# The first chunks of a gated linear attention: order of loads, decays, multiplies and small loads

## The chip, the cores and the metric

The kernel runs on one core of a Trainium2 chip. The metric is the device time of one execution in microseconds; before the change it is 438.04 (median of three runs, 437.43 to 438.84). The engines of the core work in parallel, each in its own program order, and wait for one another through semaphores: TensorE (PE in the profile, with PEld for its weight loads), VectorE (DVE), ScalarE (ACT), GpSimd (POOL), and SyncE (SP), which here only issues DMAs. ScalarE issues some DMAs too; issue work shows as ACTq and SPq.

## The reference

Two blocks follow each other. The first is a gated recurrence over 768 steps for 4 batches and 8 heads of width 48; the second sends every row to the best of 8 experts.

```python
# attention: q, k, v, alpha are (4, 8, 768, 48) float32
for t in range(S):
    state = alpha[:, :, t, :, None] * state + np.einsum('bhd,bhe->bhde', k[:, :, t], v[:, :, t])
    y[:, :, t] = np.einsum('bhd,bhde->bhe', q[:, :, t], state)
x = y.transpose(0, 2, 1, 3).reshape(3072, 384)

# experts: the best of 8 by x @ w_gate, then a two-layer network of that expert
h = np.maximum(x_sorted[lo:hi] @ w1[e], 0.0)      # w1[e]: 384 x 1024
y_sorted[lo:hi] = h @ w2[e]                       # w2[e]: 1024 x 384
out = gate_w[:, None] * y_sorted[inv_perm]
```

## The kernel before

The 3072 rows are cut into 24 chunks of 128. Within a chunk the product of the alphas up to a step is the exponential of a running sum of logarithms. So a chunk goes through these steps:

- `logs`: ScalarE takes the logarithm of alpha.
- `cums`: TensorE sums it along the steps with a triangular matrix ([...]two records each); ScalarE takes exponentials with both signs.
- `operands`: k and q are multiplied by these.
- `transposes`: TensorE transposes both products, ScalarE and VectorE copy them out of PSUM.
- `scores`: TensorE multiplies them, VectorE and ScalarE with GpSimd mask the results.
- `attend`: TensorE adds the earlier state's part, the chunk's own part, and forms the next state.
- `rows`: TensorE turns the result into rows and gate logits.

The last row of the positive exponential, the decay over the whole chunk, is stored to DRAM and loaded back with its elements on other partitions (`Eb`): `decay_out` and `decay_in`, both issued by ScalarE.

```python
def load(n, s):
    ...
    if n == "v":
        st[s][n] = vb[s % len(vb)]
        nc.sync.dma_start(st[s][n][:, :, :D], src)
    else:
        st[s][n] = ld.tile([C, H, D], F32, name=n + "_sb", bufs=5)
        nc.sync.dma_start(st[s][n][:], src)

def loads(s):
    load("k", s + 1)
    load("q", s + 1)
    load("a", s + 2)
    load("v", s)

def logs(s):
    st[s]["ln"] = work.tile([C, H, D], F32, name="ln")
    nc.scalar.activation(st[s]["ln"][:], st[s]["a"][:], AF.Ln)

def cums(s):
    d = st[s]
    cum = rps.tile([C, Dm], F32, name="cum")          # one buffer (rps has bufs=1)
    nc.tensor.matmul(cum[:], lhsT=cmask[:], rhs=d["ln"][:], start=True, stop=True)
    ...
    nc.scalar.activation(d["icp"][:], cum[:], AF.Exp, scale=-1.0)
    nc.scalar.activation(d["cp"][:], cum[:], AF.Exp)

def decay_out(s):
    if s % NB + 1 < NB:
        nc.scalar.dma_start(e_d[s : s + 1, :], st[s]["cp"][C - 1 : C, :])

def decay_in(s):
    ...
        for a in range(2):
            nc.scalar.dma_start(
                d["E"][a * DP : a * DP + D, :], e_d[s].rearrange("(p a d) -> a d p", a=2, d=D)[a],
            )

def operands(s):
    ...
    nc.gpsimd.tensor_tensor(kq[:, 0, :, :D], d["k"][:], heads(d["icp"]), op=ALU.mult)
    nc.gpsimd.tensor_tensor(kq[:, 1, :, :D], d["q"][:], heads(d["cp"]), op=ALU.mult)

def scores(s):
    ...                                               # matmuls into sA and sB
    nc.vector.tensor_tensor(d["dA"][:], sA[:], cmask[:, None, :].to_broadcast([C, NP, C]), op=ALU.mult)
    nc.scalar.copy(d["dB"][:], sB[:])
    nc.gpsimd.affine_select(d["dB"][:], d["dB"][:], ...)

def keep_busy(n):                                     # n matmuls on zeros, to fill idle time
    ...

# the start
for a in range(2):
    for ps_ in (slice(0, NP // 2), slice(NP // 2, NP)):
        ...
        nc.scalar.dma_start(gate[r0 : r0 + D, ps_], ...)      # four small loads
nc.scalar.preload_act_table_set("natural_log_exp_and_others")
for n in "akq":
    load(n, 0)
load("a", 1)
loads(0)
first_consts()
keep_busy(4)
parts = fetch_parts(0)
hots = []
for s in range(-4, NT - 1):
    if s + 5 < NT:
        loads(s + 5)
    do(attend, s)
    do(scores, s + 1)
    ...
    do(cums, s + 3)
    keep_busy({-3: 3}.get(s, 0))
    do(operands, s + 3)
    ...
    do(transposes, s + 2)
    keep_busy({-2: 2}.get(s, 0))
    if s == -1:
        back_consts()
    do(rows, s)
    do(keep_rows, s)
    do(decay_out, s + 3)
    do(decay_in, s + 2)
    do(logs, s + 4)
    ...
```

`do(f, i)` calls `f(i)` where chunk i exists, so the loop's first four turns fill a pipeline.

Of the kernel before, what the change touches and what calls it, by code (L numbers as in the profile page):

```python
# [13 lines left out]
ALU = mybir.AluOpType  # L14
# [4 lines left out]
def kernel(  # L19
# [28 lines left out]
    nc = tc.nc  # L48
    B, H, S, D = q.shape
# [3 lines left out]
    NT = N // C  # L53
# [42 lines left out]
    def at(p, a):  # L96
        return DP * (a ^ (p >= NP // 2))
# [14 lines left out]
    def first_consts():  # L112
        nc.vector.memset(still[:], 0.0)
        make_upper_triangular(nc, cmask[:], 1.0, diag=True)
        make_identity(nc, ident[:])
        nc.gpsimd.memset(back[:], 0.0)
        for t in kqb:
            nc.vector.memset(t[:, :, :, D:], 0.0)
        for t in vb:
            nc.vector.memset(t[:, :, D:], 0.0)  # L120
        for t in Ub + Eb:
            nc.vector.memset(t[:], 0.0)

    def back_consts():

        for ps_ in (slice(0, NP // 2), slice(NP // 2, NP)):
            for a in range(2):
                r0 = at(ps_.start, a)
                r = slice(r0, r0 + D)
                nc.vector.tensor_copy(  # L130
                    back[r, ps_, a * D : (a + 1) * D], ident[r, None, r0 : r0 + D].to_broadcast([D, NP // 2, D]),
                )
                nc.vector.tensor_scalar_mul(back[r, ps_, D2:], gate[r, ps_, :], -1.0)
# [100 lines left out]
    def fetch_parts(ex):  # L234

        w1 = wpools[0].tile([C, DB, F], F32, name="w1")
        w2 = wpools[0].tile([C, FB, Dm], F32, name="w2")
        w_t[ex] = w1, w2
        for a in range(DB):
            for c in range(0, F, 2 * C):  # L240
                nc.sync.dma_start(w1[:, a, c : c + 2 * C], moe_w1[ex, a * C : (a + 1) * C, c : c + 2 * C])
                yield
        for f in range(FB):
            nc.sync.dma_start(w2[:, f, :], moe_w2[ex, f * C : (f + 1) * C, :])
            yield
# [30 lines left out]
    with tc.tile_pool(name="ld", bufs=6) as ld, \  # L276
# [5 lines left out]
        def rows_of(t, s):  # L282
            b, c = s // NB, s % NB
            return t[b, :, c * C : (c + 1) * C, :].rearrange("h p d -> p h d")

        def load(n, s):
            if s >= NT:
                return
            src = rows_of({"a": alpha, "k": k, "q": q, "v": v}[n], s)
# [17 lines that stand above are left out]
        def pair(t, p):  # L307
            return t[:, 2 * p : 2 * p + 2, :].rearrange("s h d -> s (h d)")

        def heads(t):  # L310
            return t[:].rearrange("s (h d) -> s h d", h=H)

        def cums(s):
            d = st[s]
            cum = rps.tile([C, Dm], F32, name="cum")
            nc.tensor.matmul(cum[:], lhsT=cmask[:], rhs=d["ln"][:], start=True, stop=True)  # L316
            d["icp"] = work.tile([C, Dm], F32, name="icp")
            d["cp"] = work.tile([C, Dm], F32, name="cp", bufs=3)
# [11 lines that stand above are left out]
                d["E"] = Eb[s % len(Eb)]  # L330
                for a in range(2):
                    nc.scalar.dma_start(
                        d["E"][a * DP : a * DP + D, :], e_d[s].rearrange("(p a d) -> a d p", a=2, d=D)[a],
                    )

        def operands(s):
            d = st[s]
            kq = kqb[s % 4]
            nc.gpsimd.tensor_tensor(kq[:, 0, :, :D], d["k"][:], heads(d["icp"]), op=ALU.mult)  # L339
            nc.gpsimd.tensor_tensor(kq[:, 1, :, :D], d["q"][:], heads(d["cp"]), op=ALU.mult)  # L340

        def transposes(s):
            d = st[s]
            for i, n in enumerate(("kT", "qT")):
                tp = ps.tile([C, NP, C], F32, name="tp", bufs=2)
                for p in range(NP):
                    nc.tensor.transpose(tp[:, p, :], pair(kqb[s % 4][:, i], p), ident[:])  # L347
                d[n] = work.tile([C, NP, C], F32, name=n, bufs=3)
                if i:
                    nc.vector.tensor_copy(d[n][:], tp[:])  # L350
                else:
                    nc.scalar.copy(d[n][:], tp[:])
# [100 lines left out]
        def rank_products(g, pos):  # L453

            t = slice(g[0], g[-1] + 1)
            nc.tensor.matmul(pos, lhsT=ones_sq[:], rhs=ohs[:, t, :], start=True, stop=False, skip_group_check=True)
            nc.tensor.matmul(pos, lhsT=lt_strict[:], rhs=oh[:, t, :], start=False, stop=True, skip_group_check=True)
            return g, pos
# [89 lines left out]
        def do(f, i, *a):  # L548
            if 0 <= i < NT:
                f(i, *a)  # L550

        def keep_busy(n):

            if n:
                t = ps.tile([C, NP, D2 + E], F32, name="xr")[:].rearrange("r p t -> r (p t)")
            for _ in range(n):
                nc.tensor.matmul(
                    t[:, : 2 * C], lhsT=still[:, :C], rhs=still[:], start=True, stop=True, skip_group_check=True,
                )

        for a in range(2):
            for ps_ in (slice(0, NP // 2), slice(NP // 2, NP)):
                r0 = at(ps_.start, a)
                nc.scalar.dma_start(
                    gate[r0 : r0 + D, ps_], moe_w_gate.rearrange("(p a d) e -> a d p e", a=2, d=D)[a, :, ps_],
                )
        nc.scalar.preload_act_table_set("natural_log_exp_and_others")
        for n in "akq":
            load(n, 0)
        load("a", 1)  # L570
        loads(0)
        first_consts()
        keep_busy(4)
        parts = fetch_parts(0)
        hots = []
        for s in range(-4, NT - 1):
            if s + 5 < NT:
                loads(s + 5)
            do(attend, s)
            do(scores, s + 1)  # L580
            ranked = [rank_products(g, st[s]["ranks"][:, : len(g) * E]) for g in groups_of if g[-1] == s - 1]
            if s == TE + 1:
                cnt0 = st[s]["ranks"][:, :1]
                nc.tensor.matmul(
                    cnt0, lhsT=ones_sq[:], rhs=ohs[:, TE, 0:1], start=True, stop=True, skip_group_check=True,
                )
                close_early(cnt0[0:1, :])
            if s == TE + 4:
                early_slots(st[s]["ranks"][:, : EB * NQ])
            do(cums, s + 3)  # L590
            keep_busy({-3: 3}.get(s, 0))
            do(operands, s + 3)
            if s == TE + 5:
                fetch_lot(0)
            if not ranked:
                for _ in range(min(2, len(hots))):
                    one_hots(hots.pop(0))
            for r in ranked:
                slots_of(*r)
            do(transposes, s + 2)  # L600
            keep_busy({-2: 2}.get(s, 0))
            if s == -1:
                back_consts()
            do(rows, s)
            do(keep_rows, s)
            do(decay_out, s + 3)
            do(decay_in, s + 2)
            do(logs, s + 4)
            late_consts(s)
            for g in groups_of:  # L610
                if g[-1] == s:
                    choose(g)
            if s >= 8:
                next(parts, None)
                if s >= NT - 6:
                    next(parts, None)
# [3 lines left out]
        s = NT - 1  # L620
# [322 lines left out]
```

## Time and profile before

| | before |
|---|---|
| median of three runs | 438.04 us |
| span of the profiled execution | 436.7 us |
| TensorE busy | 422.0 us (97%) |
| GpSimd / VectorE / ScalarE busy | 138.9 / 147.2 / 107.1 us |
| fill matmuls at the start | 9 (18 records) |
| sums of chunks 0 to 3 begin on TensorE at | 4.67, 7.76, 12.94, 17.22 us |
| scores of chunk 0 / outputs of chunk 0 begin at | 10.43 / 14.65 us |

The time of an instruction is counted from the start of the span. "Idle before" is the time in which the instruction's engine stood still ahead of it, with what ended most of it. Stretches of idle time matter only on the engine that sets the end. A DMA's row shows only its issue on the engine that starts it; when its data landed is seen from whoever waited for it.

### The profile page before, as it was taken

How to read it: one execution, taken by the hardware profiler on the slowest of the kernel's cores; microseconds unless marked ns; L12 is line 12 of the kernel's file. 1: busy time of each engine (PE TensorE's matmuls, PEld its weight loads, DVE VectorE, ACT ScalarE, POOL GpSimd, SP SyncE). 2: the span in 40 equal slices, each digit the busy share in tenths (PEclk: the TensorE clock that was granted, in tenths of full speed). 3: DMA queues.
4: the chain of work that ended last, by engine and by line, in shares of the span. 5: the costliest groups of instructions: out<-in, count | busy, mean ns of one | idle time of the engine just before them, and what ended most of it. 6: DMA issues, size and time to landing. Idle time of an engine off the chain costs nothing.

```text
span 436.7 us, 7832 instructions
## 1 busy us (share of the span) xinstructions
PE 422.0 (97%) x2986; PEld 285.6 (65%) x2986; DVE 147.2 (34%) x454; ACT 107.1 (25%) x218; POOL 138.9 (32%) x245
## 2 busy tenths in 40 slices
PE   7899999999999999999999999999999999999992
PEld 5788888888788898655555555655655555555450
DVE  3546766766768724721011101101201101201000
ACT  4545555544453221111110111010111111111110
POOL 4567675556566350160160110033010010010010
PEclk9999999999999999999999999999999999999997
DMA  9999999999833542994542600813710230010010
GB/s 165 182 193 211 206 217 207 205 204 210 167 102 106 159 112 89 392 397 153 178 128 91 229 31 0 306 51 93 289 53 2 54 145 0 6 37 8 2 48 13
DMA packets 128433, 59.40 MB, mean 136 GB/s; under 512 B 110462, under 2 KB 123320, under 8 KB 128394
## 3 DMA queue, kind: packets, MB, share of 16 engines
q1 hardware_dynamic: 116258, 48.87, 44.3%
q0 software_dynamic: 3328, 9.94, 6.9%
q10 hardware_dynamic: 8808, 0.08, 1.2%
q8 instruction: 24, 0.39, 0.4%
q14 instruction: 15, 0.12, 0.1%
HBM read 49.30 MB, written 9.96 MB: 136 GB/s over the span
## 4 chain that ended last, share of the span: by engine, by line
PE 58%; issue 28%; POOL 4%; DMA 3%; DVE 2%; SPq 1%; ACT 1%; POOLq 0%; ACTq 0%; DVEq 0%
PE zp L800 15%; PE hp L784 13%; PE sA L360 4%; PE xr L427 4%; PE tp L347 4%; PE cum L316 4%; POOL out_dram L806 3%; PE y L397 3%; PE hp L647 2%; PE y L390 2%; PE kvp L397 2%; PE kvp L406 2%; PE xtp L776 1%; DMA k_sb<-in_k_dram 1%; POOL xg L258 1%
## 5 line engine op out<-in xcount | busy, mean ns | idle before, releaser
L800 PE MATMUL zp<-w,h_sb 128*128 128x384 f32 (+2 forms) x560 | 137.1, 487 | 0.0
L784 PE MATMUL hp<-xT,w 128*128 128x416 f32 (+3 forms) x384 | 125.1, 486 | 0.0
L800 PEld LDWEIGHTS zp<-w,h_sb 128*128 128x128 f32 (+2 forms) x560 | 73.6, 163 | 56.4 <-issue 14.8
L784 PEld LDWEIGHTS hp<-xT,w 128*128 128x128 f32 x384 | 71.7, 190 | 52.0 <-issue 37.8
L806 POOL DMA_INDIRECT out_dram<-zo,o_idx x26 | 25.9, 994 | 220.8 <-ACT zo L805 195.2
L789 DVE TENSOR_SCALAR h_sb<-hp 128x416 f32<-128x416 f32 (+3 forms) x32 | 17.9, 558 | 149.1 <-PE hp L784 142.2
L805 ACT ACTIVATE zo<-zp,gw 128x384 f32<-128x384 f32 x26 | 15.1, 581 | 123.6 <-PE zp L800 119.1
L791 ACT ACTIVATE h_sb<-hp 128x416 f32<-128x416 f32 (+3 forms) x32 | 15.7, 491 | 106.7 <-PE hp L784 102.7
L778 DVE COPY xT<-xtp 128x384 f32<-128x384 f32 (+3 forms) x29 | 13.1, 485 | 46.5 <-PE xtp L776 46.3
L360 PE MATMUL sA<-qT,kT 48*128 48x128 f32 x192 | 27.6, 284 | 0.8 <-DVE lgn L429 0.4
L258 POOL DMA_INDIRECT xg<-x_rows,g_idx x26 | 25.2, 969 | 9.2 <-issue 7.2
L360 PE MATMUL sB<-qT,kT 48*128 48x128 f32 x192 | 27.7, 285 | 0.0
L347 PEld LDWEIGHTS tp<-ident,kqb 128*128 128x128 f32 x192 | 22.4, 140 | 7.2 <-issue 4.2
L339 POOL TENSOR_TENSOR kqb<-k_sb,icp 128x384 f32<-128x384 f32 x24 | 24.1, 1006 | 9.1 <-DMA q_sb<-in_q_dram 3.9
L427 PE MATMUL xr<-back,yT 128*128 128x104 f32 x192 | 25.1, 273 | 0.0
L360 PEld LDWEIGHTS sA<-qT,kT 48*128 48x128 f32 x192 | 23.2, 187 | 2.8 <-issue 1.4
L316 PE MATMUL cum<-ln,cmask 128*128 128x384 f32 x48 | 21.8, 535 | 3.3 <-ACT ln L305 3.2
L347 PE MATMUL tp<-ident,kqb 128*128 128x128 f32 x192 | 24.9, 273 | 0.0
L340 POOL TENSOR_TENSOR kqb<-q_sb,cp 128x384 f32<-128x384 f32 x24 | 24.1, 1003 | 0.0
L427 PEld LDWEIGHTS xr<-back,yT 128*128 128x128 f32 x192 | 23.3, 192 | 0.1
L360 PEld LDWEIGHTS sB<-qT,kT 48*128 48x128 f32 x192 | 23.1, 187 | 0.0
L367 POOL TENSOR_SCALAR_AFFINE_SELECT dB<-dB 128x512 f32<-128x512 f32 x24 | 15.3, 638 | 22.5 <-ACT dB L366 22.5
(168 smaller groups left out, 474.2 us busy)
## 6 DMA issues: line engine op xcount, KB each, us to landing
w<-in_moe_w_dram SPq DMA_DIRECT2D x14, 1536.0 KB
x_rows<-xs SPq DMA_DIRECT2D x24, 196.0 KB
a_sb<-in_alpha_dram SPq DMA_DIRECT2D x24, 192.0 KB
k_sb<-in_k_dram SPq DMA_DIRECT2D x24, 192.0 KB
q_sb<-in_q_dram SPq DMA_DIRECT2D x24, 192.0 KB
vb<-in_v_dram SPq DMA_DIRECT2D x24, 192.0 KB
w<-in_moe_w_dram SPq DMA_DIRECT2D x12, 128.0 KB
w<-in_moe_w_dram SPq DMA_DIRECT2D x8, 192.0 KB
```

Of the source, the lines that this page charges most:

```text
L258: nc.gpsimd.indirect_dma_start(out=xg[:, j, :], out_offset=None, in_=x_d[: N + 1 if n else TE * C + 1, :], in_offset=bass.IndirectOffsetOn ...
L316: nc.tensor.matmul(cum[:], lhsT=cmask[:], rhs=d["ln"][:], start=True, stop=True)
L339: nc.gpsimd.tensor_tensor(kq[:, 0, :, :D], d["k"][:], heads(d["icp"]), op=ALU.mult)
L340: nc.gpsimd.tensor_tensor(kq[:, 1, :, :D], d["q"][:], heads(d["cp"]), op=ALU.mult)
L347: nc.tensor.transpose(tp[:, p, :], pair(kqb[s % 4][:, i], p), ident[:])
L360: nc.tensor.matmul(t[:, p, :], lhsT=d["kT"][r : r + D, p, :], rhs=d["qT"][r : r + D, p, :], start=True, stop=True,)
L397: nc.tensor.matmul(yp(p)[at(p, a) : at(p, a) + DP, :], lhsT=d["v"][:, 2 * p + a, :], rhs=d["d" + "AB"[a]][:, p, :], start=(c == 0 and p % ...
L427: nc.tensor.matmul(xr[:, p, :], lhsT=d["yT"][:, p, :], rhs=back[:, p, :], start=True, stop=True)
L784: nc.tensor.matmul(hp[:, c0:c1], lhsT=w1[:, a, f * C : (f + 1) * C], rhs=xT[:, a, c0:c1], start=(a == 0), stop=(a == DB - 1),)
L789: nc.vector.tensor_relu(h[:, f, c0:c1], hp[:, c0:c1])
L800: nc.tensor.matmul(zp[i * wd : (i + 1) * wd, :], lhsT=h[:, f, c : c + wd], rhs=w2[:, f, :], start=(f == 0), stop=(f == FB - 1), skip_group ...
L806: ins = nc.gpsimd.indirect_dma_start(out=out[:, :], out_offset=bass.IndirectOffsetOnAxis(ap=idx, axis=0), in_=zo[:], in_offset=None, bound ...
```

## The change

The first chunks are written out ahead of the loop instead of being run by its first turns. Alpha of chunk 1 is loaded right after alpha of chunk 0, and both chunks' decays are worked out before anything else; the multiplies of chunk 0 go to VectorE; the sums of chunks 2 and 3 both fall into the first turn of the loop, ahead of chunk 0's rows and chunk 2's transposes; five of the nine fill matmuls go and one comes (placed after chunk 0's transposes); the activation table is loaded before the gate's small loads, two of which now stand between the first two logarithms; and in the loop the logarithm goes ahead of the small decay store and loads. The purpose is that the engines take up work in the order in which its data arrives, and that a logarithm doesn't stand behind DMAs that have to wait.

```diff
-        def operands(s):
+        def operands(s, eng=nc.gpsimd):
             d = st[s]
             kq = kqb[s % 4]
-            nc.gpsimd.tensor_tensor(kq[:, 0, :, :D], d["k"][:], heads(d["icp"]), op=ALU.mult)
-            nc.gpsimd.tensor_tensor(kq[:, 1, :, :D], d["q"][:], heads(d["cp"]), op=ALU.mult)
+            eng.tensor_tensor(kq[:, 0, :, :D], d["k"][:], heads(d["icp"]), op=ALU.mult)
+            eng.tensor_tensor(kq[:, 1, :, :D], d["q"][:], heads(d["cp"]), op=ALU.mult)
 ... (the gate's four loads become gate_rows(0) and gate_rows(1), two each)
         nc.scalar.preload_act_table_set("natural_log_exp_and_others")
-        for n in "akq":
-            load(n, 0)
-        load("a", 1)
+        for n, s in (("a", 0), ("a", 1), ("k", 0), ("q", 0)):
+            load(n, s)
         loads(0)
+        gate_rows(0)
         first_consts()
         keep_busy(4)
+        logs(0)
+        gate_rows(1)
+        logs(1)
+        cums(0)
+        operands(0, nc.vector)
+        cums(1)
+        transposes(0)
+        decay_out(0)
+        loads(1)
+        operands(1)
+        keep_busy(1)
+        scores(0)
+        logs(2)
+        transposes(1)
+        decay_in(0)
+        decay_out(1)
+        loads(2)
+        back_consts()
         parts = fetch_parts(0)
         hots = []
-        for s in range(-4, NT - 1):
-            if s + 5 < NT:
-                loads(s + 5)
+        for s in range(NT - 1):
+            for n in ((3, 4, 5) if s == 0 else (s + 5,)):
+                if n < NT:
+                    loads(n)
             do(attend, s)
             do(scores, s + 1)
 ...
+            if s == 0:
+                cums(2)
+                operands(2)
+                decay_in(1)
+                decay_out(2)
+                logs(3)
 ...
             do(cums, s + 3)
-            keep_busy({-3: 3}.get(s, 0))
             do(operands, s + 3)
 ...
-            do(transposes, s + 2)
-            keep_busy({-2: 2}.get(s, 0))
-            if s == -1:
-                back_consts()
+            if s:
+                do(transposes, s + 2)
             do(rows, s)
             do(keep_rows, s)
+            if s == 0:
+                transposes(2)
+            do(logs, s + 4)
             do(decay_out, s + 3)
             do(decay_in, s + 2)
-            do(logs, s + 4)
```

More of the change, by code (lines that the diff above doesn't have):

```diff
@@ L559, in keep_busy, with gate_rows @@
                 )
-        for a in range(2):
+        def gate_rows(a):
             for ps_ in (slice(0, NP // 2), slice(NP // 2, NP)):
```

## The prediction, made before the changed kernel ran

> **What bounds the kernel now.** I read the page first: busy time by engine, then the slices.
>
> ```profile
> PE 422.0 (97%) x2986; PEld 285.6 (65%) x2986; DVE 147.2 (34%) x454; ACT 107.1 (25%) x218; POOL 138.9 (32%) x245
> ...
> PE   7899999999999999999999999999999999999992
> ...
> DMA  9999999999833542994542600813710230010010
> ```
>
> TensorE (PE) is busy nearly everywhere and executes in order, so time is won or lost only where it stands idle. The start (first slices 7 and 8) and the last slice are the thin places. Next, TensorE's timeline, read only for idle time; these are its stalls up to 21 us after the fill matmuls begin at 1.24, and one later start for comparison:
>
> ```profile
> 7.76 0.91 PE L316 MATMUL cum<-ln,cmask 128*128 128x384 f32 x2 [0.92 <-ACT ln L305]
> ...
> 12.94 0.91 PE L316 MATMUL cum<-ln,cmask 128*128 128x384 f32 x2 [1.35 <-ACT ln L305]
> ...
> 17.22 0.91 PE L316 MATMUL cum<-ln,cmask 128*128 128x384 f32 x2
> ```
>
> Columns: start, duration, instruction, idle before it and its releaser. They are the sums of chunks 1, 2 and 3. The third has no wait before it; from 12.94 on TensorE is dense (5.00 us busy in each of the windows 15 to 20, 20 to 25 and 25 to 30 us). So 17.22, the start of chunk 3's sum, is my mark: what TensorE still has to do there is the same in both kernels (chunk 0's rows and chunk 2's transposes only swap places), so a shift of this mark is a shift of the end, plus or minus later stalls.
>
> Why did chunk 2's sum wait? ScalarE's (ACT's) timeline:
>
> ```profile
> 9.62 0.23 ACTq L324 DMA_DIRECT2D decay_rows<-cp  x1
> 10.28 2.03 ACTq L332 DMA_DIRECT2D Eb<-decay_rows  x2
> 12.36 0.52 ACT L305 ACTIVATE ln<-a_sb 128x384 f32<-128x384 f32 x1 [2.30 <-DVE dA L364]
> ...
> 15.18 0.91 ACTq L332 DMA_DIRECT2D Eb<-decay_rows  x2
> 16.14 0.52 ACT L305 ACTIVATE ln<-a_sb 128x384 f32<-128x384 f32 x1 [0.84 <-DVE qT L350]
> ```
>
> The logarithm of chunk 2 stands behind two tiny loads of decay factors (Eb). The named releaser, dA, is none: the instruction follows the second issue by 0.05 us. A narrower window splits the pair into issues at 10.28 and 11.99, 0.33 us each. The compiled program says what each waits for: DMAs take eight completion semaphores in turn, and a DMA whose semaphore was used before waits for that earlier DMA to land. The first Eb load thus waits for alpha of chunk 2 (issued 5.64), the second for k of chunk 2 (issued 7.73). So these two big loads landed by about 10.25 and 11.95, 4.2 to 4.6 us after issue. Two more marks: alpha of chunk 1 landed at 7.15 (fourth load; its logarithm starts at 7.19), k of chunk 3 at about 16.0 (thirteenth; the load that waits on its semaphore goes out at 16.04). That is one load per 0.98 us ((16.0 - 7.15) / 9), as the transfer rate says:
>
> ```profile
> DMA  0039999999999999999999999944989999997199
> GB/s 0 0 55 223 203 208 196 188 193 186 187 188 194 253 208 178 179 197 220 234 187 180 190 207 242 191 63 94 196 142 211 254 201 186 221 227 127 15 176 178
> ```
>
> (40 slices of 0.75 us; 197 KB at 190 to 200 GB/s is 1.0 us.) In the first 18 us the loads are saturated: the n-th load lands near 7.15 + 0.98 (n - 4), in whatever order.
>
> Later, two stalls have the same cause, a logarithm behind Eb issues:
>
> ```profile
> 85.46 0.91 PE L316 MATMUL cum<-ln,cmask 128*128 128x384 f32 x2 [0.31 <-ACT ln L305]
> ...
> 120.24 0.91 PE L316 MATMUL cum<-ln,cmask 128*128 128x384 f32 x2 [0.66 <-ACT ln L305]
> ```
>
> The other stalls (0.36 before 40.69, 0.45 before 118.42, 0.38 before 142.43, 0.26 before 149.57 us) are of GpSimd, VectorE and of drains, which the change leaves alone.
>
> [...]
>
> **The change, part by part.**
>
> *Loads.* Order becomes alpha 0, alpha 1, k 0, q 0; the rest keeps its place. Landing by the line above: alpha 0 at about 4.0 (unchanged, its logarithm started at 4.00), alpha 1 at 5.1 instead of 7.15, k 0 6.1, q 0 7.15. Places 5 to 14 do not move: alpha 2 10.2, v 0 11.1, k 2 12, q 2 13, alpha 3 14, k 3 16, q 3 17.
>
> *Start.* Logarithm 1 at 5.1; sum 0 as before, exponentials of chunk 0 end near 6.45. There is one PSUM buffer for sums, so sum 1 runs 6.55 to 7.4 (before 7.76). VectorE multiplies k 0 at 6.2 to 6.75, q 0 at 7.2 to 7.75 (the q load decides; on GpSimd it ended 8.12). Transposes 0 end near 8.5, kT and qT by 9.2, scores 0 start at 9.35 instead of 10.43: about 1.1 us won. The four fill matmuls removed (5 fewer, 1 more) lay in idle time and bring nothing.
>
> *Up to the mark.* Scores 0 end 10.5. Transposes 1 need chunk 1's GpSimd products (k 1 8.2, q 1 9.2, done 10.2): 10.4 to 11.3. Attend 0 needs dB: ScalarE copy 10.55 to 11.15, mask on GpSimd 0.64 more: it starts 11.9, ends 13.4 (1.47 before). Scores 1 end 14.5, sum 2 ends 15.35, logarithm 2 being ready at 11.6. Here the change is ahead by 17.22 - 15.35 = 1.9 us.
>
> *The mark itself.* Sum 3 now follows sum 2 directly on TensorE. On ScalarE its logarithm stands behind: exponentials 2, Eb load pair of chunk 1, decay store of chunk 2. By the program, the decay store of chunk 1 waits for alpha 3 (14.0), so is issued at 14.1; the first Eb load of chunk 1 waits for that store to land and, by its turn of the semaphore, for q 3, the fourteenth load: 17.0, with SyncE's issues about 0.4 late (k 1 now waits for alpha 0 to land: 4.05 against 3.62) rather 17.3. Then the pair 0.91 (row at 15.18), store 0.24 and three gaps of 0.05 to 0.1: logarithm 3 at 18.5, 0.57 later (12.36 to 12.93) sum 3 at 19.1. TensorE idles 15.35 to 19.1, 3.7 us. Mark: 19.1 - 17.22 = 1.9 us later. Rows 0 and transposes 2 queue behind it, so nothing fills the hole.
>
> *Steady state.* The logarithm now goes ahead of decay store and Eb loads. Saves 0.31 + 0.66 = 0.97 at most.
>
> Sum: +1.9 - 0.97 = +0.9 us; 438.04 + 0.9 = 438.9.
>
> **Rivals.** (1) *The start gain survives*: Eb of chunk 1 does not wait for q 3. Then it waits for the store: [...] logarithm 3 at 17.9, mark 18.4, +1.2, net +0.2: 438.2. If that store is also early, net -0.5 to -1.5: 436.5 to 437.5. For it: the change is made to win here, and sum 2 does come early. Against: the trace shows such turn waits holding (10.28, 11.99). (2) *Loads as the bound*: with less in flight at the start, all loads land 0.5 to 1 us later, and the hole grows: 439.5 to 440. For it: saturated slices; against: one semaphore turn still leaves three to four loads under way. (3) *Nothing reaches the end*: later stalls take up any shift; against: from 20 us to the end only some 2.4 us of stalls exist, and the expert part is dense.
>
> **Range and chances.** Range from rival 1 with an early store (437.1) to rival 2 (440.5), widened a little for the 1.4 us spread of the three times before. All lie within 0.7%; 2% would be 8.8 us, more than the whole start region can lose or gain. Faster 0.01, same 0.98, slower 0.01.
>
> **What would show it.** Right: scores 0 near 9.4; sum 2 near 14.5; then a hole of 3 to 4 us before sum 3 with releaser ScalarE's ln; Eb of chunk 1 issued at 17 or later; no ln stalls near 85 and 120 us. Wrong: sum 3 before 17.2, or a new stall after 20 us that is larger than 1 us.

## The result, and the profile after

| | before | after |
|---|---|---|
| median of six runs | 438.84 us (437.43 to 439.2) | 441.25 us (441.14 to 441.8) |
| ratio, 95% interval | | 1.0064 [1.0049, 1.008] |
| span of the profiled execution | 436.7 us | 439.5 us |

The three times of the kernel before that the prediction knew are among its six here. The change costs 2.4 us. That is outside the predicted range: 438.9 was expected, 440.5 at most.

The page of the kernel after, busy time and slices:

```profile
PE 422.9 (96%) x2978; PEld 285.7 (65%) x2978; DVE 147.7 (34%) x456; ACT 105.6 (24%) x218; POOL 136.4 (31%) x243
...
PE   7599999999999999999999999999999999999992
...
PEclk9889999999999999999999999999999999999997
```

TensorE is as busy as before (422.0 us then). Two things are thinner: the second slice (11 to 22 us) fell from 8 to 5, and the granted clock shows 8 in the second and third slices. The timeline of TensorE in the kernel after, with the sums of chunks 1 to 4 (start, duration, instruction, idle time before it and its releaser):

```profile
6.51 0.91 PE L316 MATMUL cum<-ln,cmask 128*128 128x384 f32 x2 [0.96 <-ACT cp L320]
...
14.54 0.91 PE L316 MATMUL cum<-ln,cmask 128*128 128x384 f32 x2
20.03 1.65 PE L316 MATMUL cum<-ln,cmask 128*128 128x384 f32 x2 [4.57 <-ACT ln L305]
...
28.14 0.91 PE L316 MATMUL cum<-ln,cmask 128*128 128x384 f32 x2
```

Here and below, "sum 3" is the cumulative sum of chunk 3, and so on. Sum 2 is where the prediction put it. Then TensorE stands for 4.57 us, longer than the predicted 3.7. And the sum behind the hole lasts 1.65 us, where every other one here has 0.91. ScalarE's timeline in the kernel after says why it stands:

```profile
14.68 0.58 ACT L366 COPY dB<-sB 128x512 f32<-128x512 f32 x1 [2.57 <-PE sB L360]
15.49 0.49 ACT L319 ACTIVATE icp<-cum 128x384 f32<-128x384 f32 x1 [0.22 <-PE cum L316]
15.88 0.48 ACT L320 ACTIVATE cp<-cum 128x384 f32<-128x384 f32 x1
18.25 0.81 ACTq L332 DMA_DIRECT2D Eb<-decay_rows  x2
19.15 0.26 ACTq L324 DMA_DIRECT2D decay_rows<-cp  x1
19.45 0.52 ACT L305 ACTIVATE ln<-a_sb 128x384 f32<-128x384 f32 x1 [3.09 <-issue]
```

From 16.4 to 18.25 us ScalarE stands in front of chunk 1's small loads; the logarithm of chunk 3 is behind them in program order. The chain that ended last, in order of time, names what they wait for, and shows what the clock did next:

```profile
12.72 5.51 DMA q_sb<-in_q_dram
18.23 0.02 issue
18.25 0.31 ACTq L332
...
19.45 0.53 ACT ln L305
...
20.03 1.65 PE cum L316 x2
21.68 1.67 PE xr L427 x8
23.34 1.70 PE tp L347 x8
25.05 0.26 PE y L390 x2
```

q of chunk 3, issued at 12.72, landed at 18.23, and with it the small load's turn of its semaphore came. Behind the hole, sum 3, rows 0 and transposes 2 take 5.02 us together. In the kernel before the same three took 2.66 (17.22 to 19.88). The windows give the granted clock. A row has the window's busy time and number of records for TensorE, its weight loads, VectorE, ScalarE and GpSimd, then the granted clock, the busy share of the DMA engines and GB/s; first before, then after:

```profile
15.00:20.00 5.00, 5.00 (x72) 4.41 (x72) 4.59 (x15) 2.75 (x6) 3.31 (x5) 1.00 1.32 188
20.00:25.00 5.00, 5.00 (x78) 4.34 (x74) 2.12 (x6) 2.61 (x6) 3.08 (x8) 1.00 0.98 174
```

```profile
15.00:20.00 5.00, 0.45 (x2) 0.00 (x0) 0.95 (x2) 1.66 (x4) 2.58 (x3) 0.81 0.93 158
20.00:25.00 5.00, 4.97 (x22) 4.04 (x22) 0.19 (x1) 2.12 (x5) 2.58 (x6) 0.51 1.23 210
25.00:30.00 5.00, 5.00 (x78) 4.34 (x78) 2.53 (x6) 1.68 (x5) 1.50 (x4) 1.00 1.31 198
```

With the clock at 0.51, TensorE is "busy" in 4.97 of the 5 us from 20 to 25, although its work there takes nearly twice as long as before. A busy share alone hides this. Narrower windows of the kernel after show when the clock changed:

```profile
16.00:18.00 2.00, 0.00 (x0) 0.00 (x0) 0.27 (x1) 0.36 (x1) 1.94 (x2) 1.00 0.77 119
18.00:20.00 2.00, 0.00 (x0) 0.00 (x0) 0.69 (x2) 0.52 (x1) 0.00 (x1) 0.52 0.93 177
...
24.00:26.00 2.00, 2.00 (x29) 1.50 (x30) 0.69 (x1) 1.09 (x3) 1.00 (x5) 0.77 1.26 193
```

With a clock that is either full or half, as the trace has it here (1.00 in 16 to 18 us, 0.50 in 20 to 22 and in 22 to 24), 0.52 and 0.77 put the fall at 18.1 us, 2.6 us after sum 2 ended (14.54 + 0.91), and the return at 24.9 us, 4.9 us after sum 3 began. The shift of the kernel after against the kernel before, at equal work:

| mark on TensorE | before | after | shift |
|---|---|---|---|
| sum 3 | 17.22 | 20.03 | +2.81 |
| attend 1 (by the chain) | 19.88 | 25.05 | +5.17 |
| sum 4 | 22.97 | 28.14 | +5.17 |
| sum 8 | 46.02 | 50.75 | +4.73 |
| sum 12 | 68.62 | 73.21 | +4.59 |
| first matmul of the experts | 149.57 | 152.73 | +3.16 |
| span | 436.7 | 439.5 | +2.8 |

So 5.2 us are lost by 25 us, and 2 are regained by the experts. Of TensorE's waits of 0.2 us and more from 21 us to the experts, the kernel after has only two:

```profile
122.52 0.34 PE L360 MATMUL sA<-qT,kT 48*128 48x128 f32 x1 [0.44 <-DVE lgn L429]
...
152.73 0.70 PE L673 MATMUL hp<-xT,w 128*128 128x256 f32 x2 [0.54 <-ACT xs L434]
```

Those at 40.69, 85.46, 120.24 and 142.43 us are gone (0.36 + 0.31 + 0.66 + 0.38 = 1.71), while the last has grown by 0.28. That is 1.4 of the 2.0 us; the rest lies in shorter waits that I did not follow.

### The profile page after: what moved, and what is told of

It reads as the page before. It is cut to its first block, busy times and chain, and to the rows that moved or that the text cites. A ratio compares the mean times of both kernels' runs of the same rounds, so it can differ in the third digit from the quotient of the medians.

```text
span 439.5 us, 7814 instructions
## 1 busy us (share of the span) xinstructions
PE 422.9 (96%) x2978; PEld 285.7 (65%) x2978; DVE 147.7 (34%) x456; ACT 105.6 (24%) x218; POOL 136.4 (31%) x243
## 4 chain that ended last, share of the span: by engine, by line
PE 61%; issue 27%; POOL 4%; DMA 2%; SPq 2%; DVE 1%; ACTq 0%; ACT 0%; POOLq 0%; DVEq 0%
PE zp L826 15%; PE hp L810 13%; PE sA L360 5%; PE xr L427 5%; PE tp L347 4%; PE cum L316 4%; PE y L397 3%; POOL out_dram L832 3%; PE hp L673 2%; PE y L390 2%; PE kvp L397 2%; PE kvp L406 2%; SPq L295 1%; DMA q_sb<-in_q_dram 1%; PE xtp L802 1%
## 5 line engine op out<-in xcount | busy, mean ns | idle before, releaser
L826 PEld LDWEIGHTS zp<-w,h_sb 128*128 128x128 f32 (+2 forms) x560 | 73.5, 163 | 56.4 <-issue 14.8
L339 POOL TENSOR_TENSOR kqb<-k_sb,icp 128x384 f32<-128x384 f32 x23 | 23.1, 1002 | 13.2 <-DMA k_sb<-in_k_dram 6.3
L347 PE MATMUL tp<-ident,kqb 128*128 128x128 f32 x192 | 26.1, 279 | 0.0
L427 PEld LDWEIGHTS xr<-back,yT 128*128 128x128 f32 x192 | 24.3, 198 | 0.7 <-issue 0.6
L366 ACT COPY dB<-sB 128x512 f32<-128x512 f32 x24 | 14.0, 585 | 42.4 <-PE sB L360 27.6
L340 POOL TENSOR_TENSOR kqb<-q_sb,cp 128x384 f32<-128x384 f32 x23 | 23.0, 999 | 0.0
```

The costliest lines, as they stand in the source:

```text
L339: eng.tensor_tensor(kq[:, 0, :, :D], d["k"][:], heads(d["icp"]), op=ALU.mult)
L340: eng.tensor_tensor(kq[:, 1, :, :D], d["q"][:], heads(d["cp"]), op=ALU.mult)
L427: nc.tensor.matmul(xr[:, p, :], lhsT=d["yT"][:, p, :], rhs=back[:, p, :], start=True, stop=True)
L826: nc.tensor.matmul(zp[i * wd : (i + 1) * wd, :], lhsT=h[:, f, c : c + wd], rhs=w2[:, f, :], start=(f == 0), stop=(f == FB - 1), skip_group ...
```

## The experiments

My theory after the reading: the loop's order of logarithms is a gain; the first step of the start is the loss, because chunk 3's logarithm stands behind the small loads there; and the hole costs twice, once by its length and once by the clock after it. Rivals: the late loads alone set the end and the clock lies beside other waits; the start would be a loss in any order.

**The logarithm ahead of the small loads in the first step.**

```diff
             if s == 0:
                 cums(2)
                 operands(2)
+                logs(3)
                 decay_in(1)
                 decay_out(2)
-                logs(3)
```

> The changed kernel with one line moved: the logarithm of chunk 3 ahead of chunk 1's Eb loads and chunk 2's decay store on ScalarE. Theory (the hole before sum 3 is made by the order on ScalarE, and TensorE's granted clock falls because of the hole): logarithm 3 at about 16.4 instead of 19.45, sum 3 at about 17.0 instead of 20.03, hole 1.5 us instead of 4.57, granted clock 1.0 in the window 20 to 25 us (0.51 now), time 441.25 - 3.0 - 2.4 = about 435.8. Rival (the loads limit the start whatever the order): another wait takes its place, sum 3 after 19 us, time above 440.

Measured: 437.27 us (436.98 to 437.98), ratio 0.9959 [0.9944, 0.9975]. Four microseconds less than the kernel after, by moving one instruction past three DMA issues. TensorE's timeline of this run:

```profile
4.81 1.49 PE L316 MATMUL cum<-ln,cmask 128*128 128x384 f32 x2
7.26 1.65 PE L316 MATMUL cum<-ln,cmask 128*128 128x384 f32 x2 [0.96 <-ACT cp L320]
8.70 1.91 PE L347 MATMUL tp<-ident,kqb 128*128 128x128 f32 x8
...
16.60 0.91 PE L316 MATMUL cum<-ln,cmask 128*128 128x384 f32 x2
18.89 0.91 PE L316 MATMUL cum<-ln,cmask 128*128 128x384 f32 x2 [1.37 <-ACT ln L305]
24.64 0.91 PE L316 MATMUL cum<-ln,cmask 128*128 128x384 f32 x2
```

The hole is 1.37 us, and sum 3 takes its normal 0.91: no drop of the clock (1.00 in every window from 16 to 28 us). Sum 4 comes 3.5 us earlier than in the kernel after (24.64 against 28.14). The expected 435.8 was missed. In the profiled execution, the slowest of the six, the first products took nearly twice as long (1.49, 1.65, 1.91 us), and chunk 0's scores began at 11.48, not 9.43.

**Fill matmuls in the hole, too many.** `keep_busy` issues matmuls on zeros; in this and the next run they are extra work, and nothing is left out. On TensorE they stand between sum 2 and sum 3: the lines between give it no work.

```diff
                 decay_out(2)
                 logs(3)
+                keep_busy(18)
```

> The changed kernel with 18 fill matmuls on TensorE between sum 2 and sum 3 (18 x 0.243 = 4.4 us of work that nobody needs, inside the hole). Theory (the clock is lowered by standing idle, and costs 2.4 us on its own): sum 3 still at about 20.0, its two records 0.9 us instead of 1.65, clock 1.0 in 15 to 25 us, time 441.25 - 2.4 = about 438.8. Rival (the slow stretch after 20 us has another cause, such as the load traffic): sum 3 still takes 1.65 us, time 441.2 or more.

Measured: 442.19 us (441.72 to 443.93), ratio 1.0077 [1.0058, 1.0096]. I had mis-sized the fill: one fill matmul leaves two records, and 18 of them took 7.93 us (15.51 to 23.44), so sum 3 waited for the fill until 23.28 although its logarithm was ready at 19.72. The run still says something: sum 3 is 3.25 us later than in the kernel after, but sum 4 only 0.79 later (28.93 against 28.14), because the clock stayed at 1.00 and the work between took 2.5 us less.

**The fill at the right length.** Nine of them: 9 x 0.43 = 3.9 us.

```diff
                 decay_out(2)
                 logs(3)
+                keep_busy(9)
```

> The kernel after, with 9 fill matmuls between the sums of chunks 2 and 3 (9 x 0.432 us as the longer fill run showed = 3.9 us, so from 15.5 to 19.4 us, inside the hole that ends at 20.0). Theory (the lowered TensorE clock after the idle hole costs 2.4 us by itself): chunk 3's sum still starts at 20.0 us but takes 0.85 us and not 1.65, chunk 4's sum starts at 25.7 us and not 28.2, the clock of 20 to 25 us is about 1.0 and not 0.51; time 438.8 us, ratio to the kernel before 1.000. Rival (the lowered clock lies beside other waits, the late loads alone set the end): chunk 4's sum stays at 28 us and the time at 441.2 us, ratio 1.006.

Measured: 438.67 us (438.31 to 439.86), ratio 0.9997 [0.9985, 1.001]. TensorE's timeline of this run, and then its windows with the clock:

```profile
15.42 4.05 PE L557 MATMUL xr<-still 128*128 128x256 f32 x18
19.89 0.91 PE L316 MATMUL cum<-ln,cmask 128*128 128x384 f32 x2 [0.42 <-ACT ln L305]
...
25.64 0.91 PE L316 MATMUL cum<-ln,cmask 128*128 128x384 f32 x2
```

```profile
15.00:20.00 5.00, 4.58 (x21) 3.53 (x20) 0.96 (x2) 1.80 (x4) 2.59 (x3) 1.00 0.98 161
20.00:25.00 5.00, 5.00 (x74) 4.34 (x76) 1.64 (x4) 2.26 (x5) 2.69 (x6) 1.00 1.16 202
```

The hole is as long as ever: sum 3 comes at 19.89 (20.03 in the kernel after). But it is filled with useless work, the clock stays at 1.00, and sum 4 comes 2.50 us earlier. The time falls by 2.58 us. This isolates the clock: it costs 2.5 us, all of which reaches the end.

**What the small loads wait for.** Chunk 1's small loads read chunk 0's row of decays in place of chunk 1's, which lay in DRAM long before; chunk 1's state is thus decayed by another chunk's factors, and only the turn of the semaphore is left to wait for.

```diff
-                decay_in(1)
+                decay_in(1, 0)          # a second argument of decay_in: the row that it reads
```

> The changed kernel, but chunk 1's Eb loads read chunk 0's row of decays, so they no longer wait for chunk 1's store to land; only the wait for the earlier DMA with the same completion semaphore (q of chunk 3) is left. (Chunk 1's decays are then chunk 0's: part of the computation is changed.) If that turn of the semaphores decides: first Eb load of chunk 1 still issued at about 18.2, sum 3 at about 20.0. If the store's landing decides: issued at about 16.4, sum 3 at about 18.2.

Measured: 441.16 us (one run). ScalarE's timeline of this run:

```profile
18.02 0.81 ACTq L332 DMA_DIRECT2D Eb<-decay_rows  x2
18.92 0.26 ACTq L324 DMA_DIRECT2D decay_rows<-cp  x1
19.23 0.52 ACT L305 ACTIVATE ln<-a_sb 128x384 f32<-128x384 f32 x1 [2.66 <-issue]
```

Sum 3 comes at 19.80. Without the store to wait for, the pair still goes out only when q of chunk 3 has landed (18.00 here, 18.23 in the kernel after, where the pair went out at 18.25). So it is the turn of the semaphore, and rival 1 of the prediction falls. The hole of this run, 4.14 us, brought the lower clock as well (0.52 in 20 to 25 us).

**The loop's order alone.** The kernel before, with one line moved in the loop.

```diff
             do(keep_rows, s)
+            do(logs, s + 4)
             do(decay_out, s + 3)
             do(decay_in, s + 2)
-            do(logs, s + 4)
```

> The kernel before with one part of the change alone: in the loop the logarithm goes ahead of decay store and Eb loads (this holds for the loop's first turns too). Theory (that part is a gain in itself): logarithm 2 at about 10.3 instead of 12.36, sum 3 at about 16.2 instead of 17.22, the logarithm stalls near 85 and 120 us gone, time 438.8 - 1.0 - 1.0 = about 436.8. Rival (the gain after 28 us in the changed kernel comes only from loads having more of a lead once TensorE is late): stalls near 85 and 120 us stay, time above 437.6.

Measured: 436.40 us (435.97 to 437.02), ratio 0.9942 [0.9927, 0.9957]: faster, by 2.4 us against the 438.84 of the result, with one line. TensorE's timeline of this run, sums 2 to 4 and then all waits of 0.2 us and more that are left between 21 us and the experts' first matmul:

```profile
11.69 0.91 PE L316 MATMUL cum<-ln,cmask 128*128 128x384 f32 x2
16.44 0.91 PE L316 MATMUL cum<-ln,cmask 128*128 128x384 f32 x2
22.19 0.91 PE L316 MATMUL cum<-ln,cmask 128*128 128x384 f32 x2
```

```profile
40.07 0.18 PE L456 MATMUL kvp<-ohs,ones_sq 128*128 128x32 f16 x1 [0.44 <-POOL ohs L451]
117.17 0.34 PE L360 MATMUL sA<-qT,kT 48*128 48x128 f32 x1 [0.44 <-DVE lgn L429]
147.10 0.70 PE L647 MATMUL hp<-xT,w 128*128 128x256 f32 x2 [0.26 <-ACT xs L434]
```

Sum 3 is 0.78 us earlier than before, the experts 2.47 (147.10 against 149.57). The stalls of the logarithms at 85 and 120 are gone, and that at 142 as well (0.31 + 0.66 + 0.38 = 1.35).

**Load order, and VectorE's multiplies, in the order of steps of before.** The kernel with the loop's order, plus the two alphas loaded first; and the same with chunk 0's multiplies on VectorE.

```diff
-        for n in "akq":
-            load(n, 0)
-        load("a", 1)
+        for n, s in (("a", 0), ("a", 1), ("k", 0), ("q", 0)):
+            load(n, s)
```

> The kernel before with the loop's new order of logarithms (436.4 us, ratio 0.994, by itself) and with the two alphas loaded ahead of k and q of chunk 0. Theory (the load order brings nothing by itself: chunk 0's q then lands at 7.15 us and its GpSimd multiplies end at 8.2): the second logarithms at 5.1 us and not 7.15, scores of chunk 0 still at about 10.4 us, chunk 3's sum at 16.4 us; time 436.4 us, ratio 0.994. Rival (the load order is the part that gains): scores at 9.4 us and a time of 435.5 us or less.

Measured: 436.64 us (436.18 to 437.36), ratio 0.9949 [0.9931, 0.9967]. Scores of chunk 0 at 10.29, sum 3 at 16.53: no gain, as the theory said. One detail was wrong: the second logarithm came at 6.68 and not at 5.1, since the activation table was loaded first and chunk 0's exponentials went ahead of it.

```diff
-            nc.gpsimd.tensor_tensor(kq[:, 0, :, :D], ...)
+            eng = nc.vector if s == 0 else nc.gpsimd
+            eng.tensor_tensor(kq[:, 0, :, :D], ...)      # and the same for q
```

> The kernel before with the loop's order of logarithms, the load order of the kernel after, and chunk 0's two multiplies on VectorE (without VectorE's multiplies this took 436.6 us, scores of chunk 0 at 10.29). Theory (the multiplies bring scores forward by 1 us, but chunk 3's sum waits for its turn behind the loads and stays near 16.4 us): scores at 9.4 us, 436.4 us, ratio 0.994. Rival (the earlier scores carry through): chunk 3's sum at 15.5 us and 435.6 us, ratio 0.992.

Measured: 436.53 us (436.23 to 437.42), ratio 0.995 [0.9933, 0.9967]; scores at 10.64 and not at 9.4, sum 3 at 16.48. The time is as expected, but the run does not isolate VectorE. In before's order of steps two fill matmuls stand ahead of these scores, and in this execution the first sum took 1.62 us where it took 0.88 in the kernel before, so the scores came no earlier, and earlier scores were not tested here.

**The start in another order.** The kernel after, with both logarithms and chunk 2's sum ahead of the loop, and two fill matmuls kept.

```diff
         operands(0, nc.vector)
+        keep_busy(2)
         cums(1)
         ...
-        scores(0)
         logs(2)
+        scores(0)
         transposes(1)
         decay_in(0)
+        cums(2)
+        operands(2)
+        logs(3)
         decay_out(1)
         ...
             if s == 0:
-                cums(2)
-                operands(2)
                 decay_in(1)
                 decay_out(2)
-                logs(3)
```

> The kernel after with another order of its start: the logarithms of chunks 2 and 3 and chunk 2's sum ahead of the loop, two fill matmuls kept after chunk 0's operands, and only chunk 1's row load and chunk 2's store left in the first step. Theory (what the change lost is the order of chunk 3's logarithms behind the small loads, and the idle hole that follows): chunk 2's sum starts at about 11.5 us (14.5 in the kernel after), chunk 3's at about 15 to 16 us (20.0), no clock below 0.9 from 15 to 25 us; attend of chunk 1 may be held by its operands to about 18.5 us; time 435.5 us, ratio 0.992. Rival (with the loop's order mended, the start brings nothing more, since the late loads of the later chunks set the pace): as the kernel before with the loop's order alone, 436.4 us, ratio 0.994.

Measured: 436.19 us (435.71 to 437.95), ratio 0.9943 [0.9926, 0.996]. Sums 2 and 3 came as the theory had them (11.65, 14.96), 1.5 us ahead of the kernel with the loop's order alone at sum 3. But sum 4 was level with it: 22.21 against 22.19. ScalarE's timeline of this run shows where the lead went:

```profile
18.07 0.81 ACTq L332 DMA_DIRECT2D Eb<-decay_rows  x2
18.97 0.26 ACTq L324 DMA_DIRECT2D decay_rows<-cp  x1
19.33 0.49 ACT L319 ACTIVATE icp<-cum 128x384 f32<-128x384 f32 x1 [3.64 <-PE y L397]
```

The same wait at 18 us, this time in front of the exponentials of chunk 3. Sum 3 was over at 15.9; its exponentials came at 19.33, and TensorE then waited 0.92 us at 21.11. So I moved that wait out of the way too:

```diff
             if s == 0:
-                decay_in(1)
-                decay_out(2)
             ...
                 transposes(2)
+                decay_in(1)
+                decay_out(2)
```

> The early-sums kernel (chunk 2's sum and both logarithms ahead of the loop), with chunk 1's row load and chunk 2's store moved in the first step from ahead of chunk 3's cumulative sum to behind chunk 2's transposes. There ScalarE's queue stood at 15.1 to 18.07 us in that row load and its exponentials of chunk 3 came at 19.33. Theory (that queue wait is the same one that delays the kernel after): the exponentials of chunk 3 at about 16 us, TensorE's wait of 0.92 us at 21.11 us gone, chunk 4's sum at 21.3 us (22.21 before this edit). Whether it reaches the end: chunk 6's sum waited at 34.1 us there for logarithms behind a copy whose buffer came free with a store, so I expect most to be lost again: 436.0 us, ratio 0.994. Rival (the lead is kept): 435.3 us, ratio 0.992.

Measured: 436.43 us (435.73 to 436.86), ratio 0.9941 [0.9925, 0.9958]. The exponentials came at 16.26 and sum 4 at 21.00, 1.2 us ahead. At sum 5 it was level again (27.92 against 27.94 with the loop's order alone): among other things, a mask of GpSimd came 0.52 us late at 25.36. Sum 6 was behind (34.24 against 33.81), with TensorE waiting again. ScalarE's timeline of this run there:

```profile
33.28 0.48 ACT L434 COPY xs<-xr 128x384 f32<-128x384 f32 x1 [2.82 <-POOL first_w_i L183]
...
33.66 0.53 ACT L305 ACTIVATE ln<-a_sb 128x384 f32<-128x384 f32 x1
```

The copy of the routed rows stands from 30.46 to 33.28, which I read as a wait for a buffer: GpSimd, which writes the same buffer, waits there for the store of the rows (`x_rows<-xs`) until 32.99 (1.40 us, until 32.88, in the run ahead of this one). A third buffer takes that wait away:

```diff
-            xs = work.tile([C, W], F32, name="xs")
+            xs = work.tile([C, W], F32, name="xs", bufs=3)
```

> The same, and three buffers in place of two for the routed rows that wait for their store. Theory (the store that frees that buffer, at 32.9 us, is the next wait to end last): ScalarE's copy of chunk 2's rows no longer stands from 30.3 to 33.2 us, chunk 6's sum at 32.9 us and not 34.1, and the lead of about 1 us over the kernel before with the loop's order alone is kept to the end: 435.3 us, ratio 0.992. Rival (other waits near 40 and 117 us, for GpSimd's masks and the routing's sums, take its place): 436.1 us, ratio 0.994.

Measured: 436.52 us (435.03 to 438.27), ratio 0.9944 [0.9926, 0.9962]. The copy now goes at 30.64, sum 6 at 33.47, the wait at 40 us is gone too, and sum 12 comes at 67.03, 0.8 us ahead of the loop's order alone (67.86). Then two new waits, on TensorE's timeline of this run:

```profile
83.72 0.19 PE L456 MATMUL kvp<-ohs,ones_sq 128*128 128x32 f16 x1 [0.40 <-DVE Ub L420]
```

and 0.59 us at 94.12 for a mask of GpSimd. The experts begin at 148.45, later than the 147.10 of the loop's order alone. The rival was right about the time, though not about where.

**Two fill matmuls put back after chunk 0's multiplies,** with the logarithm ahead as in the first run of all.

```diff
         operands(0, nc.vector)
+        keep_busy(2)
         cums(1)
```

> The kernel after with chunk 3's logarithms ahead of the small loads of the first step, and two fill matmuls put back after chunk 0's operands. Theory (without them [...] the first products run at half speed): chunk 0's scores start at about 9.5 us and not at 11.5, time 435.3 to 435.8 us, ratio 0.992. Rival (the late warm-up is a matter of the execution and not of the fill matmuls): as without them, 437.3 us, ratio 0.996.

Measured: 437.25 us (436.3 to 438.35), ratio 0.9967 [0.9957, 0.9976], no different from 437.27 without them. In the profiled execution sum 1 took 0.91 and not 1.65 us, scores came at 9.86 and not 11.48, and sum 3 at 17.26 and not 18.89. That lead of 1.6 us shrank to 0.3 at the experts (148.94 against 149.23), with new waits of 0.40 and 0.28 us at 82.63 and 85.54. Two profiles don't settle whether the fill or the execution made the early products fast. The other traces speak for the execution: their records of the full clock begin at 10.74 us in the run with the logarithm ahead, but at 4.3 to 5.5 us in four more that have no such fill either (the kernel after, the row 0 run and the two with fill in the hole).

## Why the prediction was wrong

**The start and sum 2: right.** Scores of chunk 0 began at 9.43 (9.35 predicted), VectorE's multiplies took 0.56 us each at 6.22 and 7.28, against 1.00 on GpSimd (the 0.55 behind the predicted times was an estimate; a straight line through two of VectorE's products in the kernel before, 0.35 us for 192 elements, `acc`, and 0.69 for 512, `dA`, also gives 0.55 for 384), the second logarithm came at 5.11 (5.1), sum 2 at 14.54 (14.5).

**The mark: right in its mechanism, too small.** The hole came where it was predicted, with the predicted releaser, for the predicted reason; the run with row 0 shows that the semaphore's turn was the wait. The term that was mis-sized is q 3's landing, "the fourteenth load: 17.0", with SyncE's lateness "rather 17.3": it landed at 18.23, so the mark moved by 2.81 and not by 1.9. Rival 2 named 0.5 to 1 us of this, but for a reason that the trace does not bear out, a later landing of all loads: k 3 and v 1, just ahead of q 3, were in at 16.16 and 14.93, against 16.03 and 14.97 before. The trace records 16 parts of each landing. Fifteen parts of q 3 were in by 17.03 (16.89 before); only the last took until 18.23. So the rate of one load per 0.98 us held, and what it lacked is that a load is in only with its last part. Beside it stands a packet of 16 KB on the queue called `instruction`, here with its share of 16 engines from 14.9 to 15.3 us:

```profile
q8 instruction: 1, 0.02, 20.9%
```

It starts at 15.10 us and takes 1.34 us (20.9% of 16 x 0.4 us); no other packet that starts from 12 to 18 us takes over 0.18. In all eight profiles with such a packet at 14.8 to 15.6 us, the last part of q 3 comes 0.98 to 1.20 us behind the fifteenth; in the five where it starts later, 15.78 to 18.14 us, the kernel before among them, only 0.07 to 0.18. Which engine carried the packet is not recorded, so that it held up the last part is inferred, but it fits all thirteen profiles.

**The step that failed: a shift of the mark as a shift of the end.** "what TensorE still has to do there is the same in both kernels", and from it "so a shift of this mark is a shift of the end": the work is the same, its speed is not. The prediction priced the hole by its length alone. After the hole the clock was at half for 5 us, and +2.81 at sum 3 became +5.17 at sum 4. The run with nine fill matmuls shows this cost by itself, 2.58 us of time with the hole left as long as it was. By the runs, holes of 4.57 and 4.14 us brought a clock of 0.51 and 0.52, holes of 1.37 and 0.42 brought nothing (1.00 in 20 to 25 us). The clock fell 2.6 us after TensorE's last matmul here and 2.3 us after it in the row 0 run. My own predicted hole, 3.7 us, was longer than either.

**"The four fill matmuls removed lay in idle time and bring nothing": not the cause.** Putting two back did not change the time. But the reason I gave, idle time costs nothing, is the very thing that was wrong elsewhere.

**Steady state: mis-sized.** Predicted -0.97 at most; the kernel after regained 2.0 us between 25 and 150 us. The loop's order alone, in the kernel before, is worth 2.4 us. In the trace it is 2.47 by the experts: 0.78 at sum 3, where I had counted nothing for it, 1.35 in three stalls of which I had listed one (0.38 at 142.43) as untouched, and the rest in waits under 0.2 us. In the kernel after, part of what is regained is only lateness soaked up: the wait for GpSimd at 40 us is gone there, but is back (0.44) where the loop's order alone is changed.

So the sum was +1.9 - 0.97 = +0.9. Measured, in the trace, it is +2.81 for the mark, +2.36 for the clock, -2.0 by the experts, +3.2; at the end of the span 2.8, and 2.4 by the medians. The errors of the first and last terms nearly cancel (+0.9, -1.0), which is luck, so the clock is by amount the whole of the miss: without it the kernel ran in 438.67 us, against a prediction of 438.9. Two sums of the prediction were also off: the terms given for logarithm 3 (17.3 + 0.91 + 0.24 and three gaps) make 18.6 to 18.75 and not 18.5, and a range that starts at 437.1 leaves out part of rival 1's own 436.5 to 437.5.

**Rivals.** Rival 1 fell by the run with row 0. Its 438.2 rested on an estimate of mine for the landing of chunk 1's store; in the kernel after that store was in 2.9 us after its issue (14.21 to 17.14), still ahead of q 3 at 18.23. Rival 2 had the size of q 3's lateness (about 0.9) but not its reason, and its 439.5 to 440 lacked the clock too. Rival 3, later stalls taking up any shift, was dismissed too firmly. It fails for the loss, most of which reached the end. It holds for gains: six versions with the loop's order and different starts (one with a third buffer besides), with sum 3 anywhere from 14.95 to 16.53 us, had medians of 436.2 to 436.6 us. The two whose sum 3 came later, at 17.26 and 18.89 us, had 437.25 and 437.27.

Of the change, then, the one line in the loop is worth keeping, a gain of 0.6%; the rest, as it stands, costs some 5 us (441.25 against 436.40). Mended by the one line it still costs 0.9 us; mended further it brings nothing that these runs can tell from zero.

## What to carry to other kernels

- When a change opens a hole on TensorE, add up its length and ask whether it is long enough to lower the clock: here the clock fell 2.6 us into a hole of 4.57 us and cost another 2.5 us after it, and filling the hole with work on zeros bought those back. Read the granted clock next to the busy share, which showed 4.97 of 5 us at half speed.
- Put instructions that others wait for ahead of DMA issues that may have to wait on the same engine; a DMA's wait can be for a transfer that has nothing to do with it, by its turn of the semaphores (the pair of the row 0 run went out at 18.02, when q of chunk 3 had landed at 18.00). One moved line won 2.4 us in the kernel before, and 4 in the kernel after.
- An earlier start of a pipeline is worth only what the next waits leave: follow the lead from mark to mark before counting it.

## What the runs showed of the hardware

- After a hole of 4.57 us the granted clock was 0.51 in 20 to 25 us and matmul groups took about twice as long (1.65 us for 0.91; 1.67 for the rows and 1.70 for the transposes on the chain, against 0.87 each); by 25 us it was back at 1.00.
- The first products of an execution can take nearly twice as long or not: with the same instructions up to there, sum 1 took 0.91 us in the kernel after and with nine fill matmuls, and 1.65 in the run with the logarithm ahead. The trace's records of the full clock begin at 4.43, 5.43 and 10.74 us in these three; before that the windows print 1.00 for want of a record.
- A load of 0.8 KB took long among saturated loads: issued at 13.16 us in the kernel after, its reader on VectorE, idle for 3.74 us until then, began at 17.73. That is some 4.5 us from issue to use. Fifteen of its 16 parts were in by 16.26, the last at 17.61, late as q 3's last part was.
